# Attention and a gated feed-forward block in one kernel: output groups of seven 384-column products instead of two times seven 192-column ones

## The chip, the cores and the metric

The kernel runs on one core of a Trainium2 chip. The metric is device time in microseconds; the time given for a kernel is the median of its runs. Engines that matter here: TensorE (PE: matrix products, whose results lie in PSUM), VectorE (DVE), ScalarE (ACT), GpSimd (POOL) and SyncE (SP, whose queue issues most stores and all transposing transfers).

## The reference

Eight batches of twelve heads, 448 tokens, head size 64, go through softmax attention; the result, 3584 tokens of width 768, goes through a feed-forward block with two input weights of 768 x 1536 and one output weight of 1536 x 768.

```python
def _attn_ref(q, k, v):
    scores = (1.0 / np.sqrt(q.shape[-1])) * np.matmul(q, k.transpose(0, 1, 3, 2))
    attn = np.exp(scores - np.max(scores, axis=-1, keepdims=True))
    attn = attn / (np.sum(attn, axis=-1, keepdims=True) + 1e-09)
    return np.matmul(attn, v)

def _moe_ref(x, w_gate, w_val, w_out):
    g = x @ w_gate
    silu = g * (1.0 / (1.0 + np.exp(-g)))
    return silu * (x @ w_val) @ w_out
```

Inputs and output are float32; the kernel multiplies in float16 and accumulates in float32.

## The kernel before

**Stages.** Attention works on 48 pairs of heads. For each pair TensorE forms transposed scores (tile `s`, L346 to L376), ScalarE takes their exponential into `E` (L366, L384), and TensorE multiplies by the values with a column of ones (tile `acc`, L402 to L438). VectorE divides (`pv_close`), and the 128-column results are turned into `X`, by SP's transposing DMAs for the later pairs (`turn_x`, L525 and L529). A second stream, the feed-forward block, is laid between: its tokens come in blocks of 384 and 512 by turns. A *step* (`class Step`) is one of the twelve 128-row slices of the hidden layer for a block: six products for the gate (`gp`, L588), a tanh on ScalarE (`sg`, L615), six products for the value (`vp`), two VectorE operations (L641, L647) that write `hts`. The last block of 512 and the last 896 tokens use `Unit`, in which the same products are done by Winograd's form of Strassen's method, with seven half-size products in place of eight; an ordering planner (`order_of`) puts those in line.

**Output groups.** The output product, `hts` times `wo`, is done for most tokens by the same seven-product scheme. A *pair* is two chunks of 128 tokens. Its 2 x 2 blocks are (first or second chunk) x (first or second half of the 1536 hidden rows) on the left, and on the right (half of the hidden rows) x (two column ranges). The sums of the left blocks are made by VectorE (`h_sums`, L571 to L574, in `Hall`), those of the right blocks once (`out_sums`, in `Tsum`). Before the change the 768 output columns are taken as two *groups* (`qw` 0 and 1) of 384 columns, each of whose 2 x 2 blocks has 192 columns. `out_group` (L699 and on) runs one: all of its products are 128 x 192 (L710), and their accumulators `a`, `c` and `b` lie in one tile `og` of the `ps_s` pool, `a` and `c` in its first bank and `b` in its second. Each of the seven products is six matmuls. Around them:

- ScalarE (or VectorE, if `own`) copies `a` to `p1` (L754, L756), VectorE adds `c` to give `p15` (L757);
- VectorE writes `p15 + b` back to `c` (L759), reads the next `b` with `p15` to `osb` (L763), and the last `b` with `p1` (L773);
- ScalarE copies `a` and `c` together to `osb` (L735); `store` (L671) issues the DMAs, for the whole 768 columns when the second group ends.

`out_group` is a generator with two stops, so that the callers lay other work in: `run_group` a step inside, `run_groups` two groups of a pair in turn.

**Order.** Everything is written out by hand: instructions stand on each engine in the order of the calls. The loop over `plan` makes visits of three score tiles each, then the values of a pair that is due (in most visits), then feed-forward work. From visit `base` on, the list `VISITS` tells it: (block that begins, steps, groups, plain output slices, sums on VectorE at the end). A visit without values is called bare. Two steps at the end of a visit are run as `run_pair`, with the last one's value in two halves. `sums` is a queue of VectorE operations, taken one at a time by `add_sum`.

PSUM has two pools: `ps_s` with three buffers of two banks (scores, gates, groups) and `ps_f` with two of one bank (value accumulators `acc`, `vp`, plain outputs `op`). A buffer is handed out again in turn when its last reader is done.

After the visits come the last pair of heads, the units of the last block of 512 (`x5`), then three pairs of groups (one left over and `groups5`), the units of the last 896 tokens, and three final pairs, the last of which (`last`) stores each piece as soon as it is there, over two queues.

Of the kernel before, what the change touches and what calls it, by code (L numbers as in the profile page):

```python
# [16 lines left out]
HS = 4096.0  # L17
# [48 lines left out]
def kernel(  # L66
# [487 lines left out]
    def out_sums(c):  # L554
        b11, b12, b21, b22 = (
            wo_all[:, :, ds(f, 2), ts(i, QW)].rearrange("p h c m -> p c h m") for f in (c, NH + c) for i in range(2)
        )
        t1, t2, t3, t4 = (t[:, ds(c, 2)].rearrange("p c (h m) -> p c h m", h=2) for t in Tsum)
        return [
            lambda: nc.vector.tensor_sub(t1, b12, b11),  # L560
            lambda: nc.vector.tensor_sub(t2, b22, t1),
            lambda: nc.vector.tensor_sub(t3, b22, b12),
            lambda: nc.vector.tensor_sub(t4, b21, t2),
        ]
# [138 lines left out]
    def out_group(kk, c0, hts, t, at, qw, osb, last=False, own=False, mid=None):  # L703
        x, y, w = ts(2 * t, 128), ts(2 * t + 1, 128), ts(qw, QW)
        g = ps_s.tile([128, 2, 512], FP32, tag="s", name="og")
        a, c, b = g[:, 0, 0:QW], g[:, 0, QW:OH], g[:, 1, 0:QW]

        def product(dst, lhs, rhs, first=False):
            return [
                nc.tensor.matmul(  # L710
                    dst, lhsT=lhs(n), rhs=rhs(n), start=first and n == 0, stop=n == NH - 1, skip_group_check=True
                )
                for n in range(NH)
            ]

        def hh(half, z):
            return lambda n: hts[:, half * NH + n, z]

        def hs(m):
            return lambda n: Hall[at][m][:, n]  # L720

        def bb(oh, half):
            return lambda n: wo[qw][:, half * NH + n, ts(oh, QW)]

        def tt(m):
            return lambda n: Tsum[m][:, n, w]

        def out_part(z, src):
            if last and qw:
                halves = [osb[z][:, ds(qw * OH + x * QW, QW)] for x in range(2)]  # L730
                return [
                    nc.scalar.activation(halves[0], src[:, 0:QW], AF.Copy, scale=1.0 / HS),
                    nc.vector.tensor_scalar_mul(halves[1], src[:, QW:], 1.0 / HS),
                ]
            return [nc.scalar.activation(osb[z][:, ts(qw, OH)], src, AF.Copy, scale=1.0 / HS)]  # L735

        def stored(z, lo=0, w=OH):
            l0 = c0 + (2 * t + z) * 128
            if last:
                store(osb[z], kk, l0, 128, qw * OH + lo, w, (nc.sync, nc.scalar), True)  # L740
            elif qw and not lo:
                store(osb[z], kk, l0, 128, 0, DM)

        def apart(mms, *others):
            for mm in mms:
                for other in others:
                    tc.declare_no_dep(mm.ins, other.ins, reason="another bank")

        product(a, hh(0, x), bb(0, 0), True)
        product(c, hh(0, y), tt(0))  # L750
        p1 = fp.tile([128, QW], FP32, tag="p1", name="p1")
        p15 = fp.tile([128, QW], FP32, tag="p15", name="p15")
        if own:
            keep1 = nc.vector.tensor_scalar_mul(p1[:], a, 1.0 / HS)  # L754
        else:
            keep1 = nc.scalar.activation(p1[:], a, AF.Copy, scale=1.0 / HS)  # L756
        keep15 = nc.vector.scalar_tensor_tensor(p15[:], c, 1.0 / HS, p1[:], ALU.mult, ALU.add)  # L757
        apart(product(b, hs(0), tt(1), True), keep1, keep15)
        nc.vector.scalar_tensor_tensor(c, p15[:], HS, b, ALU.mult, ALU.add)  # L759
        yield  # L760
        product(b, hs(1), tt(2))
        d = osb[1][:, ds(qw * OH + QW, QW)]
        part = nc.vector.scalar_tensor_tensor(d, b, 1.0 / HS, p15[:], ALU.mult, ALU.add)  # L763
        if last:
            stored(1, QW, QW)
        if mid:
            mid()
        apart(product(a, hh(1, x), bb(0, 1)), part)
        apart(product(c, hs(2), bb(1, 1)), part)
        row0 = out_part(0, g[:, 0, 0:OH])  # L770
        stored(0)
        apart(product(b, hh(1, y), tt(3)), *row0)
        nc.vector.scalar_tensor_tensor(osb[1][:, ds(qw * OH, QW)], b, 1.0 / HS, p1[:], ALU.mult, ALU.add)  # L773
        stored(1, 0, QW if last else OH)
        yield

# [145 lines left out]
    with tc.manual_schedule():  # L922
# [50 lines left out]
        def pair_groups(kk, c0, hts, t, last=False, at=None):  # L973
            at = t if at is None else at
            osb = []

            def begin(qw, own=False, mid=None):
                if not qw:
                    osb.extend(new_osb() for _ in range(2))
                return out_group(kk, c0, hts, t, at, qw, osb, last, own, mid)  # L980

            return [(lambda own=False, mid=None, qw=qw: begin(qw, own, mid), h_sums(hts, t, at) if not qw else []) for qw in range(2)]

        def add_block(i, visits):
# [18 lines left out]
            groups.extend(x for t in range(1 + odd) for x in pair_groups(kk, c0, hts, t))  # L1003
# [3 lines left out]
            sums.extend(groups[0][1])  # L1007
            later = [f for _, fs in groups[1:] for f in fs]
            groups[:] = [(begin, []) for begin, _ in groups]
            sums.extend(later)  # L1010

# [3 lines left out]
            (2, 2, 0, 0, 2), (0, 2, 0, 0, 3), (0, 1, 1, 0, 0), (0, 2, 0, 0, 0), (0, 1, 1, 0, 0),  # L1015
            (0, 2, 0, 0, 0), (0, 1, 1, 0, 0), (0, 2, 0, 0, 0), (0, 1, 1, 0, 0), (3, 2, 0, 0, 1),
            (0, 2, 0, 0, 1), (0, 1, 1, 0, 0), (0, 0, 0, 1, 0), (0, 2, 0, 0, 0), (0, 0, 0, 1, 0),
            (0, 1, 1, 0, 0), (0, 0, 0, 1, 0), (0, 2, 0, 0, 0), (0, 0, 0, 1, 0), (0, 2, 0, 0, 0),
            (4, 2, 0, 0, 1), (0, 2, 0, 0, 1), (0, 1, 1, 0, 0), (0, 1, 0, 0, 0), (0, 1, 1, 0, 0),
            (0, 1, 0, 0, 0), (0, 1, 1, 0, 0), (0, 1, 0, 0, 0), (0, 1, 1, 0, 0), (0, 1, 0, 0, 0),  # L1020
# [84 lines left out]
        def run_group(nf, inside=None, gate_first=False, sum_between=True):  # L1105
            gen = groups.pop(0)[0](gate_first)
            for _ in range(nf - 1):
                run_fv()
            step = fvq.pop(0)
            if gate_first:  # L1110
                step.gate()
                add_sum()
            next(gen)
            if not gate_first:
                step.gate()
                add_sum(sum_between)
            if inside:
                inside()
                next(gen)
            step.value(0)  # L1120
            step.finish()
            if not inside:
                next(gen)
            add_sum()
# [367 lines left out]
```

## Time and profile before

| | |
|---|---|
| median of 3 runs | 427.63 us (427.6 to 427.68) |
| the profiled execution's own time | 427.29 us |
| its span, first to last instruction | 425.5 us |
| PE busy | 419.2 us, 4796 matmuls |
| output groups on PE (L710) | 924 matmuls |
| DVE, ACT, POOL busy | 271.1, 244.9, 229.8 us |
| stage from the first group to the last visit | 133.58 to about 298 us |
| three pairs behind the units of the last 512-block | 327.75 to 348.4 us |
| three final pairs | 400.3 to 421.3 us |

The columns of the profile's rows: line of the kernel, engine, operation, output and input tiles (buffer numbers left out), shape, and `xN` for N instructions merged into one row. In a timeline each row begins with its start and its length in us; in the chain of waits likewise, by engine, tile and line. "PEld" is the loading of a matmul's stationary operand, which overlaps the products. A matmul's end is modelled, so that the lengths of neighbours overlap; the distance between starts is what a product costs TensorE.

### The profile page before, as it was taken

What the parts mean: (1) busy time and instruction counts of PE and PEld (TensorE: products, weight loads), DVE (VectorE), ACT (ScalarE), POOL (GpSimd) and SP (SyncE); (2) the same over time, 40 slices, a digit from 0 to 9 for tenths busy, and PEclk for the clock granted to TensorE, in tenths of its full rate; (3) what the DMA queues carried; (4) which work ended last, traced back from release to release, by engine and by line L of the source; (5) the groups of instructions that cost most, each with busy time, mean ns of one, the idle gap of its engine ahead of it and who ended that gap; (6) DMA issues with size and microseconds to landing.
All of it is one profiled execution on the core that took longest, in us unless ns stands there. A gap on an engine that the chain in (4) does not pass through costs nothing.

```text
span 425.5 us, 11944 instructions
## 1 busy us (share of the span) xinstructions
PE 419.2 (99%) x4796; PEld 292.0 (69%) x4796; DVE 271.1 (64%) x644; ACT 244.9 (58%) x395; POOL 229.8 (54%) x351
## 2 busy tenths in 40 slices
PE   8999999999999999999999999999999999999996
PEld 3766666655557777757766777777889985555795
DVE  4666572785669656575635776677777765665663
ACT  6975667646755654656666546559654235545221
POOL 8656614997887774468733876935999000000000
PEclk9999999999999999999999999999999999999999
DMA  9999999999999999999999998723101231000125
GB/s 136 182 200 200 199 175 190 136 177 215 115 138 143 124 176 121 141 146 129 119 148 136 151 144 106 139 46 94 23 2 29 87 114 36 0 2 1 39 75 149
DMA packets 107928, 49.79 MB, mean 117 GB/s; under 512 B 59872, under 2 KB 104672, under 8 KB 107872
## 3 DMA queue, kind: packets, MB, share of 16 engines
q0 software_dynamic: 46800, 24.56, 52.3%
q1 hardware_dynamic: 60752, 24.22, 30.9%
q8 instruction: 37, 0.61, 0.6%
q10 hardware_dynamic: 320, 0.25, 0.2%
q14 instruction: 19, 0.16, 0.1%
HBM read 49.55 MB, written 11.01 MB: 142 GB/s over the span
## 4 chain that ended last, share of the span: by engine, by line
PE 92%; ACT 4%; DVE 2%; DMA 0%; issue 0%; ACTq 0%; DVEq 0%
PE og L710 17%; PE gp L588 17%; PE vp L588 12%; PE un L833 10%; PE acc L438 8%; PE ub L833 8%; PE s L346 5%; PE op L681 5%; PE acc L402 2%; PE s L376 2%; ACT E L366 2%; PE s L358 1%; ACT E L384 1%; PE tp L317 1%; PE wp L164 1%; PE op L1039 1%
## 5 line engine op out<-in xcount | busy, mean ns | idle before, releaser
L366 ACT ACTIVATE E<-s 128x896 f16<-128x896 f32 x126 | 106.6, 918 | 40.2 <-PE s L346 28.3
L588 PE MATMUL gp<-X,wg 128*128 128x384 f16 (+1 forms) x360 | 74.0, 347 | 0.0
L238 POOL COPY qk<-qkraw 128x512 f16<-128x512 f16 x70 | 43.4, 666 | 55.2 <-DMA qkT<-qk 55.0
L588 PE MATMUL vp<-X,wv 128*128 128x384 f16 (+3 forms) x360 | 66.7, 321 | 0.1
L641 DVE SCALAR_TENSOR_TENSOR t<-sg,gp 128x384 f32<-128x384 f32 (+1 forms) x60 | 36.1, 607 | 41.7 <-ACT sg L615 41.6
L588 PEld LDWEIGHTS <-wv 128*128 128x128 f16 x462 | 43.7, 98 | 25.8 <-issue 0.3
L588 PEld LDWEIGHTS <-wg 128*128 128x128 f16 x360 | 32.8, 98 | 26.2 <-issue 1.9
L178 POOL DMA_DIRECT2D vraw<-in_v_dram x72 | 44.3, 643 | 9.4 <-DVE X L523 8.5
L615 ACT ACTIVATE sg<-gp 128x384 f32<-128x384 f32 (+1 forms) x60 | 32.1, 537 | 27.9 <-PE gp L588 27.4
L178 POOL DMA_DIRECT2D qkraw<-in_k_dram x70 | 42.8, 631 | 6.5 <-DMA wo<-in_moe_w_out_dram 4.0
L384 ACT ACTIVATE E<-s 112x896 f16<-112x896 f32 x48 | 40.5, 917 | 7.9 <-PE s L376 7.8
L438 PEld LDWEIGHTS <-E 128*128 128x128 f16 (+2 forms) x1224 | 38.0, 98 | 10.1 <-issue 4.0
L710 PEld LDWEIGHTS <-hts 128*128 128x128 f16 x528 | 44.1, 98 | 0.3
L438 PE MATMUL acc<-vo,E 128*128 128x65 f16 (+2 forms) x1224 | 42.4, 193 | 0.1
L647 DVE SCALAR_TENSOR_TENSOR hts<-t,vp 128x384 f16<-128x384 f32 (+3 forms) x60 | 32.5, 541 | 5.8 <-PE vp L588 1.9
L481 DVE TENSOR_TENSOR xt<-acc,R 128x256 f16<-128x256 f32 x72 | 30.6, 425 | 2.5
L735 ACT ACTIVATE osb<-og 128x384 f32<-128x384 f32 x21 | 10.3, 490 | 37.9 <-PE og L710 37.9
L201 POOL DMA_DIRECT2D qkraw<-in_q_dram x43 | 29.6, 688 | 4.3 <-DMA vraw<-in_v_dram 1.4
L346 PE MATMUL s<-qkT 64*64 64x448 f16 (+1 forms) x288 | 30.8, 354 | 0.4
L710 PE MATMUL og<-wo,hts 128*128 128x192 f16 x264 | 29.0, 246 | 0.0
L710 PEld LDWEIGHTS <-hsum 128*128 128x128 f16 x300 | 25.6, 98 | 1.0
L219 DVE COPY vo<-vraw 128x512 f16<-128x512 f16 (+1 forms) x48 | 21.8, 457 | 3.0 <-DMA vraw<-in_v_dram 2.9
(184 smaller groups left out, 708.8 us busy)
## 6 DMA issues: line engine op xcount, KB each, us to landing
vraw<-in_v_dram POOLq DMA_DIRECT2D x72, 64.0 KB, 4.9
qkraw<-in_q_dram POOLq DMA_DIRECT2D x39, 112.0 KB, 4.2
qkraw<-in_k_dram POOLq DMA_DIRECT2D x68, 64.0 KB, 4.7
wg<-in_moe_w_gate_dram POOLq DMA_DIRECT2D x8, 288.0 KB, 9.8
wv<-in_moe_w_val_dram POOLq DMA_DIRECT2D x8, 288.0 KB, 10.4
wo<-in_moe_w_out_dram POOLq DMA_DIRECT2D x2, 1152.0 KB, 19.2
out_dram<-osb SPq DMA_DIRECT2D x7, 288.0 KB, 3.7
out_dram<-osb SPq DMA_DIRECT2D x6, 336.0 KB, 3.4
```

The costliest lines, as they stand in the source:

```text
L178: eng.dma_start(dst[ts(s, 64)], rows)
L238: nc.gpsimd.tensor_copy(dst.rearrange("p c h d -> p h c d"), src)
L346: nc.tensor.matmul(s[ts(half, m), hx, 0:S], lhsT=t[ts(hx, 64), ds((c + low(pr, hx)) * 128 + half * m, m)], rhs=t[ts(hx, 64), ds(NC * 128, S)],
L366: nc.scalar.activation(e[:, 0 : 2 * S].rearrange("p (h q) -> p h q", h=2), s[:, :, 0:S], AF.Exp, scale=sm_scale)
L384: nc.scalar.activation(e[:, :, 0:S], s[0:P, :, 0:S], AF.Exp, scale=sm_scale)
L438: nc.tensor.matmul(acc[ds(lo, m), ts(j, D + 1)], lhsT=e[rows, ds(hx * S + j * 128 + lo, m)], rhs=Vts[pr % NV][rows, hx, col, 0 : D + 1], s ...
L588: nc.tensor.matmul(dst[:, 0:w], lhsT=wslice(kind, self.fb, cb), rhs=X[kk][:, cb, ds(c0 + lo, w)], start=(cb == 0), stop=(cb == NCB - 1),)
L615: self.readers = [nc.scalar.activation(self.sg[:, 0:n], gp[:, 0:n], AF.Tanh, scale=0.5)]
L641: nc.vector.scalar_tensor_tensor(self.t1[:, 0:n], self.sg[:, 0:n], 1.0, self.gp[:, 0:n], ALU.add, ALU.mult)
L647: nc.vector.scalar_tensor_tensor(self.hts[:, self.fb, ds(lo, w)], self.t1[:, ds(lo, w)], 0.5 * HS, vp[:, 0:w], ALU.mult, ALU.mult)
L710: nc.tensor.matmul(dst, lhsT=lhs(n), rhs=rhs(n), start=first and n == 0, stop=n == NH - 1, skip_group_check=True)
L833: mm = nc.tensor.matmul(dst, lhsT=lhs[:, n], rhs=rhs[:, n], start=first and n == 0, stop=n == NK - 1, skip_group_check=True,)
```

## The change

All groups become wide ones: a pair is one group, whose 2 x 2 blocks have 384 columns. `out_group` and `pair_groups` give way to a class `OutPair` with a method `wide`; accumulators `a` and `c` have a bank each in one `ps_s` tile, and `b` lies in a `ps_f` buffer (in the last pair in two halves, in a second `ps_s` tile). `p1` and `p15` have 384 columns, one buffer each in the visits, and the tiles `kept` at the end. Nothing is laid inside a group but up to four VectorE sums. In `VISITS`, five visits hold a group and no step, and five that held a group now have no group and one step more; the visits' totals of steps are the same. The early opening of value accumulators behind a group (`after_group`) goes, and so does the variant with values inside a group (`run_group_with`). `out_sums` pairs the columns as halves of 384.

```diff
@@ out_sums
-        b11, b12, b21, b22 = (
-            wo_all[:, :, ds(f, 2), ts(i, QW)].rearrange("p h c m -> p c h m") for f in (c, NH + c) for i in range(2)
-        )
-        t1, t2, t3, t4 = (t[:, ds(c, 2)].rearrange("p c (h m) -> p c h m", h=2) for t in Tsum)
+        b11, b12, b21, b22 = (wo[i][:, ds(f, 2)] for f in (c, NH + c) for i in range(2))
+        t1, t2, t3, t4 = (t[:, ds(c, 2)] for t in Tsum)
@@ out_group -> OutPair.wide
-        g = ps_s.tile([128, 2, 512], FP32, tag="s", name="og")
-        a, c, b = g[:, 0, 0:QW], g[:, 0, QW:OH], g[:, 1, 0:QW]
...
+        def wide(self, keep, add_sum, ns=(1, 2, 1)):
+            osb = self.open()
+            g = ps_s.tile([128, 2, 512], FP32, tag="s", name="og")
+            a, c = g[:, 0, 0:OH], g[:, 1, 0:OH]
+            if self.last:
+                bs = ps_s.tile([128, 2, 512], FP32, tag="s", name="ob")
+                parts = [(i * QW, QW, bs[:, i, 0:QW]) for i in range(2)]
+            else:
+                parts = [(0, OH, ps_f.tile([128, 512], FP32, tag="f", name="ob")[:, 0:OH])]
...
+            product(a, self.hh(0, self.x), self.bb(0, 0, 0, OH), True)
+            keep1 = nc.scalar.activation(p1, a, AF.Copy, scale=1.0 / HS)
+            apart(product(c, self.hh(0, self.y), self.tt(0, 0, OH), True), keep1)
+            done = [nc.vector.scalar_tensor_tensor(p15, c, 1.0 / HS, p1, ALU.mult, ALU.add)]
+            for lo, w, b, mms in products(self.hs(0), 1, True):
+                done.append(combine(c, p15, HS, b, lo, w))
+            add_sum(ns[0])
+            apart(product(a, self.hh(1, self.x), self.bb(0, 1, 0, OH)), *done)
+            left = nc.scalar.activation(osb[0][:, 0:OH], a, AF.Copy, scale=1.0 / HS)
...
+            if self.last:
+                self.stored(0, 0, OH, both)
+            for lo, w, b, mms in products(self.hs(1), 2):
+                combine(osb[1][:, OH:], b, 1.0 / HS, p15[:, ds(lo, w)], lo, w)
+            if self.last:
+                self.stored(1, OH, OH, both)
+            add_sum(ns[1])
+            apart(product(c, self.hs(2), self.bb(1, 1, 0, OH)), left)
+            nc.scalar.activation(osb[0][:, OH:], c, AF.Copy, scale=1.0 / HS)
...
+            for lo, w, b in parts:
+                mms = product(b, self.hh(1, self.y), self.tt(3, lo, w))
+                apart(mms, *ends)
+                ends.append(combine(osb[1], b, 1.0 / HS, p1[:, ds(lo, w)], lo, w))
+                if self.last:
+                    self.stored(1, lo, w, both)
+            if not self.last:
+                self.stored(1)
+            add_sum(ns[2])
@@ VISITS
-            (2, 2, 0, 0, 2), (0, 2, 0, 0, 3), (0, 1, 1, 0, 0), (0, 2, 0, 0, 0), (0, 1, 1, 0, 0),
-            (0, 2, 0, 0, 0), (0, 1, 1, 0, 0), (0, 2, 0, 0, 0), (0, 1, 1, 0, 0), (3, 2, 0, 0, 1),
-            (0, 2, 0, 0, 1), (0, 1, 1, 0, 0), (0, 0, 0, 1, 0), (0, 2, 0, 0, 0), (0, 0, 0, 1, 0),
-            (0, 1, 1, 0, 0), (0, 0, 0, 1, 0), (0, 2, 0, 0, 0), (0, 0, 0, 1, 0), (0, 2, 0, 0, 0),
-            (4, 2, 0, 0, 1), (0, 2, 0, 0, 1), (0, 1, 1, 0, 0), (0, 1, 0, 0, 0), (0, 1, 1, 0, 0),
-            (0, 1, 0, 0, 0), (0, 1, 1, 0, 0), (0, 1, 0, 0, 0), (0, 1, 1, 0, 0), (0, 1, 0, 0, 0),
+            (2, 2, 0, 0, 2), (0, 2, 0, 0, 3), (0, 0, 1, 0, 0), (0, 2, 0, 0, 0), (0, 2, 0, 0, 0),
+            (0, 2, 0, 0, 0), (0, 0, 1, 0, 0), (0, 2, 0, 0, 0), (0, 2, 0, 0, 0), (3, 2, 0, 0, 1),
+            (0, 2, 0, 0, 1), (0, 0, 1, 0, 0), (0, 0, 0, 1, 0), (0, 2, 0, 0, 0), (0, 0, 0, 1, 0),
+            (0, 2, 0, 0, 0), (0, 0, 0, 1, 0), (0, 2, 0, 0, 0), (0, 0, 0, 1, 0), (0, 2, 0, 0, 0),
+            (4, 2, 0, 0, 1), (0, 2, 0, 0, 1), (0, 0, 1, 0, 0), (0, 1, 0, 0, 0), (0, 2, 0, 0, 0),
+            (0, 1, 0, 0, 0), (0, 0, 1, 0, 0), (0, 1, 0, 0, 0), (0, 2, 0, 0, 0), (0, 1, 0, 0, 0),
             (5, 0, 0, 1, 0), (0, 0, 0, 2, 0), (0, 0, 0, 0, 0),
@@ run_group
+        def run_group():
+            pair = groups.pop(0)
+            keep = [fp.tile([128, OH], FP32, tag=tag, bufs=1, name=tag) for tag in ("p1", "p15")]
+            pair.wide(keep, add_sum, (1, 1, 0))
@@ score tiles of a visit
-                if n == 2 and (after_group or ordered[n] in quads):
+                if n == 2 and ordered[n] in quads:
                     rests = open_products(rests, small)
@@ the groups behind the units
-                one, two = (begin(mid=add_sum) for begin, _ in pair)
-                next(one)
-                add_sum()
-                for gen in (two, one, two):
-                    next(gen)
-                add_sum()
+            for n, pair in enumerate(pairs):
+                pair.wide(kept[2 * (n % 2) : 2 * (n % 2) + 2], add_sum)
```

## The prediction

> **What bounds the kernel now.** I read the page's busy line, its slices and its chain first, and then the timeline of the stages where the output groups stand.
>
> ```profile
> PE 419.2 (99%) x4796; PEld 292.0 (69%) x4796; DVE 271.1 (64%) x644; ACT 244.9 (58%) x395; POOL 229.8 (54%) x351
> PE   8999999999999999999999999999999999999996
> PEclk9999999999999999999999999999999999999999
> PE 92%; ACT 4%; DVE 2%; DMA 0%; issue 0%; ACTq 0%; DVEq 0%
> PE og L710 17%; PE gp L588 17%; PE vp L588 12%; PE un L833 10%; PE acc L438 8%; PE ub L833 8%; PE s L346 5%; PE op L681 5%; PE acc L402 2%; PE s L376 2%; ACT E L366 2%; PE s L358 1%; ACT E L384 1%; PE tp L317 1%; PE wp L164 1%; PE op L1039 1%
> ```
>
> TensorE is in hand at full granted clock, and 92% of the chain is its work; the output groups (og, L710) are the largest line of it. So there are only three ways to move the time: fewer nanoseconds for the same products, less waiting of TensorE, or a shorter end. The chain of waits gives the pace of narrow products and of 384-column ones, here from two stages:
>
> ```profile
> 152.86 1.95 PE gp L588 x12
> 327.75 20.79 PE og L710 x252
> ```
>
> 20.79/252 = 82.5 ns for 192 columns, 1.95/12 = 162.5 ns for 384. Two narrow ones cost 165.0, so a wide one saves 2.5 ns; and 252 in a row at that pace means that the groups themselves wait for nothing today. The small waits stand behind them. TensorE's timeline, first behind a narrow group, then behind a pair of steps, then in a visit with a single step:
>
> ```profile
> 138.50 0.66 PE L710 MATMUL og<-qkraw,hts 128*128 128x192 f16 x6
> 139.09 0.38 PE L358 MATMUL s<-qkT 64*64 64x448 f16 x4
> 139.30 0.76 PE L346 MATMUL s<-qkT 64*64 64x448 f16 x8
> 139.99 2.12 PE L588 MATMUL gp<-X,wg 128*128 128x384 f16 x12
> ...
> 176.46 0.55 PE L346 MATMUL s<-qkT 64*128 64x448 f16 x4
> 176.85 0.28 PE L438 MATMUL acc<-vo,E 64*128 64x65 f16 x8
> 177.05 0.36 PE L346 MATMUL s<-qkT 64*128 64x448 f16 x2
> 177.34 0.91 PE L438 MATMUL acc<-vo,E 128*128 128x65 f16 x24
> 178.09 1.24 PE L588 MATMUL gp<-X,wg 128*128 128x512 f16 x5
> ```
> ```profile
> 169.41 0.74 PE L346 MATMUL s<-qkT 64*128 64x448 f16 x6
> 169.99 1.12 PE L438 MATMUL acc<-vo,E 64*128 64x65 f16 x32
> 170.95 0.25 PE L710 MATMUL og<-wo,hts 128*128 128x192 f16 x1
> ```
>
> Behind a pair of steps, scores and values take 169.41 to 170.95 = 1.54 us; behind a narrow group 176.46 to 178.09 = 1.63. In the visit without values, scores take 139.09 to 139.99 = 0.90 against 0.59 in others (0.21 for L358, 0.38 for the eight of L346): the second and third score tiles wait for the narrow group's and the step's PSUM tiles.
>
> **The change, part by part.**
>
> *The products.* Eleven pairs of token chunks, two narrow groups each, 7 products of 6 matmuls: 924 narrow. After: ten pairs of 42 wide, and the last pair, whose three T products are in halves, 24 wide and 36 narrow. 924 x 82.5 = 76.23 us; 444 x 162.5 + 36 x 82.5 = 75.12. All of it is on the path: **-1.1 us**, 0.53 of it in the five pairs of the visits, 0.58 in the six at the end.
>
> *Inside a wide group.* The b bank is written three times, with one product of another bank (6 x 162.5 = 0.975 us) between uses, in which VectorE must read it. No 384-wide combine of this kind stands in the trace; the nearest rows are L641 and L647, the same operation at 384 columns, 553 ns (192-wide combines 353 to 363). A product's modelled end lies 0.163 behind the next product's start (0.246 long, 0.0825 spacing), VectorE began 0.04 behind that (419.13 + 0.66 to 419.83), and TensorE 0.04 behind VectorE (268.22 to 268.26). So the return is 0.163 + 0.04 + 0.553 + 0.04 = 0.80 of 0.975: hidden, 0.18 to spare. Ahead of it in VectorE's order stand the two closings of the values (2 x (0.176 + 0.425) = 1.2 us, done about 1.05 behind the group's start by the rows at 255.59); the token sums (0.55) are emitted behind a combine and are done before the next one is due. ScalarE's first copy can come behind the third exponential, at about 1.4, ends at 1.9, and p15 is due at 2.15. I take 0, with 0.1 a return (20 returns, 2 us) as the far bound; a gain is excluded, as the groups wait for nothing now.
>
> *The visits.* Ten visits held a step and a narrow group or so (2, 4, 6, 8, 11, 15, 22, 24, 26, 28 of the list VISITS, counted from 0; 2 begins at 132.0, 28 at 278.7); now 2, 6, 11, 22, 26 hold a group alone and 4, 8, 15, 24, 28 have one step more. The same 12 steps of each block remain. Visits that followed a narrow group and now follow a pair of steps (5, 9, 16, 25, 29) should take 1.54 instead of 1.63: 0.09 each. Visit 3 loses its 0.31, because the group's tile now holds only a and c, and c is copied out (0.49) while the last product (0.975) runs. Visits 7, 12, 23, 27 follow a wide group: b now lies in the two-buffer pool that the value accumulators use, so the second accumulator waits for b's last combine, free at 0.80 behind the last product, where scores are through at 0.09 + 0.58 + 0.03 = 0.70 (0.09: the four products before 139.09 take 2.08, not 1.98). That is 0.10, about the 0.09 that these visits waste today. In 16, 25 and 29 the next thing late is ScalarE (chain of waits, in the visit after a group):
>
> ```profile
> 264.28 2.41 ACT E L366 x3
> 266.69 0.04 issue
> 266.74 0.50 ACT sg L615
> 267.24 0.02 issue
> 267.26 0.56 DVE t L641
> 267.83 0.02 issue
> 267.85 0.37 DVE hts L647
> ```
>
> Three exponentials, the gate's tanh and two VectorE operations set when the next score tile is free (268.26); TensorE arriving 0.09 earlier waits 0.09 longer. So I count 0.31 + 2 x 0.09: **-0.5 us**, between 0 and the 1.1 that ten visits waste today (0.31 + 9 x 0.09).
>
> *Stores and VectorE's other work.* Each pair's eight or so stores on SP now go out one to four visits earlier. Behind them in SP's order stand the transposes of keys and values; a burst of four stores took 2.6 us (264.66), while the last key transpose is issued at 275.08, lands about 5 later and is first read at 292.84. That cover of over 10 us hides it. Per pair VectorE falls from 8 x 0.357 to 4 x 0.553 us and ScalarE from 1.65 to 1.47: neither on the path. The weight sums keep their sizes and their order: nothing.
>
> *The end.* VectorE and the stores behind the last product:
>
> ```profile
> 420.62 0.66 PE L710 MATMUL og<-qkraw,hts 128*128 128x192 f16 x6
> ...
> 421.41 0.36 DVE L733 TENSOR_SCALAR osb<-og 128x192 f32<-128x192 f32 x1 [1.22 <-DMA out_dram<-osb]
> 421.68 0.35 DVE L773 SCALAR_TENSOR_TENSOR osb<-og,p 128x192 f32<-128x192 f32 x1
> ```
>
> The last product ends at 421.28, its combine begins at 421.68 behind L733, which waited for a store, and the last of the stores goes out near 422.2, 0.92 behind the product. After, L733 is gone (ScalarE copies 384 columns while the last halves of b are multiplied): combine from 0.04 to 0.40, store at 0.43; the store before it, at about -0.07, takes some 0.4 of each queue and does not hold it. **-0.45 us**, between 0 and 0.5.
>
> **Sum:** -1.1 - 0.5 - 0.45 = -2.05 us. The profiled execution took 427.29 (span 425.5 and 1.8 around it), 0.34 under the median of 427.63; 425.2 on its own scale is 425.6 on the median's.
>
> **Rivals.**
>
> *The chain through ScalarE eats the visits.* If, as in visit 25 (from 263.88), exponentials pace most visits from 2 to 29, TensorE's 0.53 + 0.5 there become waits: -0.58 - 0.45 = -1.0, 426.6. For it: three of the visits are paced so. Against: a group visit gives 6.8 us of products to 2.5 of exponentials, and a pair visit 3.9 or more.
>
> *The b bank turns round too slowly* (slower). If anything stands ahead of the combine on VectorE when b is ready, say one token sum of 0.55, the return is 1.35 and TensorE waits 0.38; at 20 returns 7.5 us, 433.1. It decides from a return of 1.08 on (20 x 0.10 eats the 2.05). For it: narrow groups had a step or a second group between their halves, and this cover is gone. Against: the order of emission puts sums behind the combines, and the margin of 0.18 is a third of an operation.
>
> The Trainium skill speaks for that rival twice, in Perfetto Trace Analysis: under Optimizing Tensor Performance, independent groups should rotate through banks so that reading one overlaps the products of the next, and under Optimizing Scalar/DVE Operations, breaking instructions up can let work finish sooner where VectorE or ScalarE cause TensorE's bubbles. The trace so far has no bubble in the narrow groups and gives the 0.18 above, so that by these rules the sum would be the rival's, and by the rows it stays at -2.05.
>
> *Nothing to be measured.* Twenty returns late by 0.05 and the four visits behind wide groups waiting 0.2 instead of 0.1 give back 1.4 of the 2.05: 427.0.
>
> **How the numbers follow.** 0.2% (0.86 us) is about what a measurement of this kernel can tell from no change. Forecast 0.60, its own range 424.6 to 426.2; the chain through ScalarE 0.19; nothing 0.08; the slow bank 0.13. The first two are faster: 0.79. The low end of the range takes all bounds at their best (-1.1 - 1.1 - 0.5 = -2.7) and 0.4 more for prices too high, 424.5; the high end takes in the second case and most of the third, 427.3. Outside are the slow bank and a little at each end, under 0.2.
>
> **What would show it.** Right: L710's successor with 480 matmuls, wide ones at 162.5 ns in unbroken runs of 42; visit 3's scores at 0.59; the last store about 0.45 behind the last product. Wrong: gaps of TensorE ahead of the second or third product into ob; values behind a wide group waiting more than 0.2 for VectorE; exponentials back to back over several visits; or a key transpose that lands after its visit has begun.

## The result, and the profile after

The change makes the kernel faster by 0.3%: 426.31 us (median of 11 runs, 425.87 to 427.19) against 427.6 for the kernel before on the same chip (11 runs, 427.05 to 427.89). The ratio is 0.9971, 95% interval 0.9962 to 0.998, that is 0.9 to 1.6 us. The forecast was 425.6. The direction was right, and the time lies in the whole range of 424.5 to 427.3, but 0.1 outside the forecast's own part of it (424.6 to 426.2), on the side of its first rival; the gain of 2.05 us was forecast too large by 0.8. The profiled execution took 426.09 us, its span 424.31, 1.19 less than the span before.

The page of the kernel after, with the busy line, the clock and the chain:

```profile
PE 417.6 (98%) x4382; PEld 263.7 (62%) x4382; DVE 265.2 (63%) x606; ACT 243.5 (57%) x385; POOL 229.6 (54%) x351
PEclk9999999999999999999999999999999999999999
PE 93%; ACT 3%; DVE 2%; DMA 1%; issue 1%; SPq 0%; DVEq 0%; ACTq 0%
```

TensorE has 1.6 us less work and still bounds the kernel at the full granted clock. The chain of waits in the three pairs behind the units, where no other work lies between:

```profile
327.30 1.95 PE og L703 x12
329.25 0.97 PE ob L703 x6
330.23 0.98 PE og L703 x6
...
334.13 1.95 PE og L703 x12
```

A wide product takes 162.5 ns (0.975 for six), and three b products alternate with the others without a gap: a group takes 6.83 us here. The next table lays the stages of both profiled executions side by side, measured from the starts of the first matmuls.

| stage | before | after | measured | forecast |
|---|---|---|---|---|
| start to the first group | 133.58 | 133.60 | 0 | 0 |
| first group to the units of the last 512-block | 164.58 | 164.10 | -0.48 | -0.53 products, -0.5 waits |
| three pairs behind those units | 20.79 | 20.47 | -0.32 | with the next but one, -0.58 |
| both stretches of units, 29.4 and 51.95 | 81.37 | 81.39 | +0.02 | 0 |
| first to last matmul start of the final pairs | 20.71 | 20.47 | -0.24 | (above) |
| last matmul's start to VectorE's end | 1.00 | 0.64 | -0.36 | -0.35 |
| VectorE's end to the end of the span | 3.47 | 3.63 | +0.16 | -0.1 |

So the products gave what they should, the visits' small waits gave nothing in sum, and the end gave less than half. TensorE's timeline of the kernel after shows the visits: behind the first wide group, through the visit without values and its pair of steps, to the next scores and values.

```profile
139.45 1.14 PE L703 MATMUL ob<-qkraw,hts 128*128 128x384 f16 x6
140.52 0.38 PE L358 MATMUL s<-qkT 64*64 64x448 f16 x4
140.73 0.55 PE L346 MATMUL s<-qkT 64*64 64x448 f16 x8
141.21 2.12 PE L586 MATMUL gp<-X,wg 128*128 128x384 f16 x12
...
145.23 0.86 PE L346 MATMUL s<-qkT 64*128 64x448 f16 x6
145.92 1.19 PE L438 MATMUL acc<-vo,E 64*128 64x65 f16 x32
146.94 0.81 PE L586 MATMUL gp<-X,wg 128*128 128x384 f16 x4
```

Scores in the visit without values take 140.52 to 141.21 = 0.69 (0.90 before): a gain, though not down to the 0.59 of the forecast. But scores and values of the next visit take 145.23 to 146.94 = 1.71, where the same visit took 1.54 before (144.01 to 145.55). Summed over all visits of this stage, the times of scores and values come to the same 47.45 us before and after. The gains, 0.69 together (-0.21 here, -0.08 to -0.09 each in visits 5, 9, 16 and 29, the rest in small pieces), are paid back in others: +0.18 in visit 4 and +0.06 to +0.09 in each of 15, 17, 25 and 30, 0.48 together, and +0.04 to +0.06 in each of the four behind wide groups (7, 12, 23 and 27), 0.20 together. Visits are counted from 0 at the first entry of `VISITS`; TensorE's part of a visit begins with its scores.

### The profile page after: what moved, and what is told of

It reads as the page before. It is cut to its first block, busy times and chain, and to the rows that moved or that the text cites. A ratio compares the mean times of both kernels' runs of the same rounds, so it can differ in the third digit from the quotient of the medians.

```text
span 424.3 us, 11026 instructions
## 1 busy us (share of the span) xinstructions
PE 417.6 (98%) x4382; PEld 263.7 (62%) x4382; DVE 265.2 (63%) x606; ACT 243.5 (57%) x385; POOL 229.6 (54%) x351
## 4 chain that ended last, share of the span: by engine, by line
PE 93%; ACT 3%; DVE 2%; DMA 1%; issue 1%; SPq 0%; DVEq 0%; ACTq 0%
PE gp L586 18%; PE vp L586 12%; PE un L855 10%; PE og L703 10%; PE acc L438 8%; PE ub L855 8%; PE ob L703 8%; PE s L346 5%; PE op L679 4%; PE acc L402 2%; PE s L376 2%; ACT E L384 1%; PE s L358 1%; ACT E L366 1%; PE tp L317 1%; PE op L1049 1%
## 5 line engine op out<-in xcount | busy, mean ns | idle before, releaser
L238 POOL COPY qk<-qkraw 128x512 f16<-128x512 f16 x70 | 42.8, 655 | 57.3 <-DMA qkT<-qk 56.0
L586 PE MATMUL gp<-X,wg 128*128 128x384 f16 (+1 forms) x360 | 73.1, 348 | 0.0
L586 PE MATMUL vp<-X,wv 128*128 128x384 f16 (+3 forms) x360 | 64.2, 314 | 0.1
L586 PEld LDWEIGHTS <-wv 128*128 128x128 f16 x492 | 46.1, 98 | 24.5 <-issue 0.4
L703 PEld LDWEIGHTS <-hts 128*128 128x128 f16 x270 | 25.9, 98 | 15.9
L645 DVE SCALAR_TENSOR_TENSOR hts<-t,vp 128x384 f16<-128x384 f32 (+3 forms) x60 | 31.4, 523 | 5.6 <-PE vp L586 2.1
L481 DVE TENSOR_TENSOR xt<-acc,R 128x256 f16<-128x256 f32 x72 | 30.6, 425 | 2.5
L201 POOL DMA_DIRECT2D qkraw<-in_q_dram x43 | 29.4, 685 | 4.2 <-DMA vraw<-in_v_dram 1.5
L346 PE MATMUL s<-qkT 64*64 64x448 f16 (+1 forms) x288 | 29.2, 353 | 0.5 <-DVE hts L645 0.2
L703 PE MATMUL og<-wo,hts 128*128 128x384 f16 x132 | 25.1, 326 | 0.0
L480 DVE RECIPROCAL R<-acc 128x4 f32<-128x4 f32 x72 | 12.7, 177 | 17.7 <-PE acc L438 17.5
L219 DVE COPY vo<-vraw 128x512 f16<-128x512 f16 (+1 forms) x48 | 19.7, 413 | 3.4 <-DMA vraw<-in_v_dram 3.4
L679 PE MATMUL op<-wo,hts 128*128 128x192 f16 (+1 forms) x168 | 21.4, 281 | 0.0
```

Of the source, the lines that this page charges most:

```text
L238: nc.gpsimd.tensor_copy(dst.rearrange("p c h d -> p h c d"), src)
L346: nc.tensor.matmul(s[ts(half, m), hx, 0:S], lhsT=t[ts(hx, 64), ds((c + low(pr, hx)) * 128 + half * m, m)], rhs=t[ts(hx, 64), ds(NC * 128, S)],
L586: nc.tensor.matmul(dst[:, 0:w], lhsT=wslice(kind, self.fb, cb), rhs=X[kk][:, cb, ds(c0 + lo, w)], start=(cb == 0), stop=(cb == NCB - 1),)
L679: nc.tensor.matmul(op[:, 0:w], lhsT=hts[:, fb, ts(ch, 128)], rhs=wo[oh][:, fb, ds(off, w)], start=fb == 0, stop=fb == NFB - 1,)
L703: nc.tensor.matmul(dst, lhsT=lhs(n), rhs=rhs(n), start=first and n == 0, stop=n == NH - 1, skip_group_check=True)
```

## The experiments

**Wide sums, narrow products.** Everything as after, but each wide product is issued as two of 192 columns.

```diff
     def product(dst, lhs, rhs, first=False):
+        w = dst.shape[1]
+        step = min(w, QW)
         return [
             nc.tensor.matmul(
-                dst, lhsT=lhs(n), rhs=rhs(n), start=first and n == 0, ...
+                dst[:, ds(lo, step)], lhsT=lhs(n), rhs=rhs(n)[:, ds(lo, step)],
+                start=first and n == 0 and lo == 0, ...
             )
+            for lo in range(0, w, step)
             for n in range(NH)
```

> The changed kernel with each wide product issued as twice six 192-column matmuls into the same accumulators; order, VISITS, VectorE and ScalarE work, PSUM tiles and stores are those of the changed kernel. Theory (the gain is 2.5 ns for each matmul saved, and the new arrangement of the visits is worth nothing): 444 wide matmuls become 888 narrow ones, 444 x (165.0 - 162.5) = +1.1 us over the changed kernel, about 427.4; the lead over the kernel before at the end of the visits, 0.40 us, falls to about 0; what is left of the gain is the end, 0.2 us. Rival (the gain comes from the arrangement, from fewer waits and fewer VectorE and ScalarE operations): no more than 0.2 us slower than the changed kernel, about 426.4, and the lead of 0.40 stays.

Measured: 428.3 us (427.99 to 429.62), ratio to the kernel before 1.0018 (1.0006 to 1.0029). In the stages against the kernel after: visits +0.54, three pairs +0.32, final pairs +0.26, together 1.1, which is the 444 x 2.5 ns of the forecast; a group in the visits takes 7.02 instead of 6.92. The visits' stage is then 164.64, against 164.58 in the kernel before: with narrow products the new arrangement of the visits is worth nothing. The span is 2.22 longer than that of the kernel after (426.53 against 424.31), and the other 1.1 us of this lie elsewhere: 0.38 ahead of the first group, a stretch that differed by up to 0.65 between the profiled executions of all these kernels, and some 0.7 behind the last matmul, where SP's and ScalarE's queues were held longer by their stores. ScalarE's two stores behind the last group's first half, of this kernel and then of the kernel after:

```profile
419.34 2.25 ACTq L669 DMA_DIRECT2D out_dram<-osb  x2
```

```profile
417.85 1.54 ACTq L669 DMA_DIRECT2D out_dram<-osb  x2
```

The last copy of c stands behind them in ScalarE's order, and they took 2.25 instead of 1.54. Why is not settled. The product term of the forecast is confirmed where it was placed.

**Values in halves behind a wide group.** The second accumulator waits there for b's last combine; that wait has cover if the values are taken as in the visits ahead of the first group: the first accumulator's full rows, then the last rows of both, then the second's full rows, and not the last rows of both first.

```diff
-            split = 0 <= base - x < 3
+            split = 0 <= base - x < 3 or (x > base and VISITS[x - 1 - base][2] > 0)
```

> The changed kernel, but in a visit behind a wide group the values of the first head are multiplied into the first accumulator before the second accumulator is touched. Theory (the 0.12 us that the values lose behind a wide group are the second accumulator's wait for the last combine of b; behind that, exponentials pace the visits with a plain output slice or a single step): scores and values of visits 7, 12, 23 and 27 fall from 1.71, 1.71, 1.66 and 1.67 us to about 1.55 to 1.6; the visits behind 12 and 27 give their share back, so that the lead at the end of the visits grows by 0.1 to 0.25 us, and the time to about 426.1. Rival (the 0.12 is a cost of switching from products to scores and values, not a wait): no visit changes by over 0.03 us.

Measured: 426.88 us (426.0 to 430.45), ratio 0.9987 (0.9966 to 1.0007): no gain. The four visits became 1.75 to 1.77 instead of 1.66 to 1.71, 0.29 us more together. TensorE's timeline in one of them, here and then in the kernel after:

```profile
165.39 0.55 PE L346 MATMUL s<-qkT 64*64 64x448 f16 x8
165.87 1.24 PE L438 MATMUL acc<-vo,E 128*128 128x65 f16 x32
166.94 0.81 PE L586 MATMUL gp<-X,wg 128*128 128x384 f16 x4
```

```profile
165.19 0.55 PE L346 MATMUL s<-qkT 64*64 64x448 f16 x8
165.58 1.27 PE L438 MATMUL acc<-vo,E 64*64 64x65 f16 x40
166.68 1.14 PE L586 MATMUL gp<-X,wg 128*128 128x384 f16 x6
```

In the kernel after, the matmul that opens the second accumulator at 165.70 comes 118 ns behind the one ahead of it, when b's combine (VectorE, 165.09 to 165.65) is through. That wait, forecast as 0.10, is gone in the split form. But the split form changes between matmuls over 64 rows and over 128 rows twice more, and each change shows as 121 to 125 ns between two starts. The wait was as forecast, but this cure costs more than it saves: neither the theory (1.55 to 1.6) nor the rival (no change) came about.

**The last stores.** The last pair's second half goes out as one 384-column store behind both combines, not as two.

```diff
-                if self.last:
-                    self.stored(1, lo, w, both)
-            if not self.last:
+            if self.last:
+                self.stored(1, 0, OH, both)
+            else:
                 self.stored(1)
```

> The changed kernel, but the last row block's left half is stored by one pair of DMAs behind both halves instead of a pair behind each. Theory (the last store is held by its queue, which issues one per 0.4 to 0.47 us, and not by the combine): the last pair of stores goes out within 0.1 us of the end of the last combine (0.15 to 0.25 in the changed kernel), and the end comes 0.05 to 0.15 us earlier in spite of twice the bytes. Rival (the end is set by how long the last store takes to land): later by 0.1 us or more, as 147 KB instead of 74 KB land last.

Measured: 426.47 us (425.98 to 428.28), ratio 0.9971 (0.9956 to 0.9986), the same as the kernel after. The last store is issued 0.03 us behind the last combine instead of 0.23, but the last landing comes 2.42 behind that issue instead of 2.18, and the span ends 3.81 behind VectorE instead of 3.63. So the queue's hold is real, some 0.2, and a larger last transfer takes it back and 0.18 more, which is the rival's sign; this is one profile of each, and the medians do not tell the two kernels apart.

Its profile showed something else, in the first wide group: 7.27 us instead of 6.92. The chain of waits there:

```profile
134.98 0.54 DVE qkraw L569
...
135.64 0.43 DVE xt L481
...
136.12 1.15 PE ob L703 x6
```

The first product into b waits for the closing of a value accumulator (L481), because b takes its buffer. VectorE came to it late, since two sums ahead of it were long. Its rows, and GpSimd's:

```profile
132.68 0.89 DVE L570 TENSOR_TENSOR hts<-hts 128x768 f16<-128x768 f16 x1
133.60 0.85 DVE L571 TENSOR_TENSOR hsum<-hts 128x768 f16<-128x768 f16 x1
134.48 0.56 DVE L572 TENSOR_TENSOR hsum<-hts,hsum 128x768 f16<-128x768 f16 x1
```

```profile
132.54 1.49 POOL L238 COPY qk<-qkraw 128x512 f16<-128x512 f16 x2 [3.15 <-DMA qkT<-qk]
```

In the kernel after, the same sums take 0.55 and 0.56, and GpSimd's copies lie before them (130.47 to 131.64).

**Half of the exponentials' work.** To see whether ScalarE's chain ate the visits' gain, the exponentials of the later stages cover half their columns, in both kernels; the other half of the attention weights is left out.

```diff
+        w = S if len(ering) <= ER else S // 2
         nc.scalar.activation(
-            e[...].rearrange("p (h q) -> p h q", h=2), s[:, :, 0:S], AF.Exp, scale=sm_scale
+            e[...].rearrange("p (h q) -> p h q", h=2)[:, :, 0:w], s[:, :, 0:w], AF.Exp, scale=sm_scale
```

> The kernel before with each exponential of the pairs from the thirteenth on (L366) taken over half of its columns: half of the attention weights are left out, and ScalarE needs about 0.57 us instead of 0.92 for each. All theories: waits of TensorE for score tiles behind the single steps (about 0.3 us each, three times) and behind the plain output slices (0.1 to 0.25 us each) shrink or go; those behind narrow groups, 0.09 us each, stay; 1 to 3 us faster than the kernel before. It is there for the comparison with the changed kernel under the same cut.

> The changed kernel with the same cut: each exponential of the pairs from the thirteenth on over half of its columns, so half of the attention weights are left out. Theory (the exponentials' chain took what the new arrangement of the visits would have given: 0.18 and 0.08 us behind the bare visits with a pair of steps, 0.06 to 0.09 behind plain output slices and single steps): with ScalarE's work halved these go, and the lead over the kernel before under the same cut, at the end of the visits, is 0.7 to 0.9 us instead of 0.40; the whole difference 1.5 to 1.8 us. Rival (the visits' gain never existed: TensorE's own switching costs and VectorE's return time are the same): the lead at the end of the visits is 0.35 to 0.5 us as before the cut, the whole difference 1.2 us.

> The changed kernel with each exponential of the pairs from the thirteenth on over half of its columns, so half of the attention weights are left out; profiled once more, since the first profile was at half the granted clock and tells nothing of the visits. Against the kernel before under the same cut, the theory (the exponentials' chain took the visits' gain) wants a lead of 0.7 to 0.9 us at the end of the visits, and the 0.18 us behind visit 3 and the 0.08 behind visit 24 gone; the rival (that gain never existed) a lead of 0.35 to 0.5 and the same 0.18 and 0.08.

Measured: before with the cut 427.16 us (426.94 to 428.1), ratio to the whole kernel before 0.9987 (0.9976 to 0.9997), which is 0.6 us and not the expected 1 to 3; after with the cut 425.5 beside it (ratio 0.9947, 0.993 to 0.9964) and 425.4 in a second comparison (0.995, 0.9936 to 0.9963), whose profile is read here. Without the exponentials' length the change is worth 427.16 - 425.5 = 1.66 us instead of 1.29. The intervals are too wide to tell these two apart; the visits do. Their stage falls from 164.21 to 163.12, by 1.09 instead of 0.48. Of this 0.51 are the times of scores and values (46.98 against 46.47 us), which without the cut gained nothing; about 0.1 stands in the first group's visit of the kernel before, which took 5.60 instead of 5.51 in this profile. Counted from the start of the span the lead is only 0.64, under the expected 0.7 to 0.9, since the first group began 0.45 later in this profile of the kernel after. TensorE's timeline with the cut, where the kernel after had 1.71:

```profile
145.58 0.74 PE L346 MATMUL s<-qkT 64*128 64x448 f16 x6
146.16 1.12 PE L439 MATMUL acc<-vo,E 64*128 64x65 f16 x32
147.12 1.14 PE L587 MATMUL gp<-X,wg 128*128 128x384 f16 x6
```

145.58 to 147.12 is 1.54, so the loss of 0.18 in visit 4 is gone, and that of 0.08 in visit 25 too (1.54); visits 15, 17 and 30 are the same in both cut kernels. The visits behind wide groups keep their 1.66 to 1.71, as they should, since b's combine and not ScalarE is late there. ScalarE's own rows say how it comes about, of the kernel after and of the cut one:

```profile
140.98 2.54 ACT L366 ACTIVATE E<-s 128x896 f16<-128x896 f32 x3 [0.84 <-PE s L358]
143.38 0.90 ACT L613 ACTIVATE sg<-gp 128x384 f32<-128x384 f32 x2
145.64 1.73 ACT L366 ACTIVATE E<-s 128x896 f16<-128x896 f32 x2 [1.36 <-PE s L346]
```

```profile
141.33 1.42 ACT L367 ACTIVATE E<-s 128x448 f16<-128x448 f32 x3 [0.84 <-PE s L358]
142.75 0.49 ACT L614 ACTIVATE sg<-gp 128x384 f32<-128x384 f32 x1
143.72 0.49 ACT L614 ACTIVATE sg<-gp 128x384 f32<-128x384 f32 x1 [0.48 <-PE gp L587]
```

Uncut, three exponentials run to 143.5 and both gates' tanhs follow back to back behind them; cut, the second tanh waits 0.48 for TensorE, so that ScalarE has time to spare. VectorE's rows of the kernel after show what TensorE waits for in visit 4:

```profile
145.33 0.35 DVE L645 SCALAR_TENSOR_TENSOR hts<-t,gp 128x192 f16<-128x192 f32 x1
145.59 0.35 DVE L645 SCALAR_TENSOR_TENSOR hts<-t,vp 128x192 f16<-128x192 f32 x1
```

They read the two halves of the last step's value: the first half lies in the `ps_s` buffer of its gate, the second in a `ps_f` buffer. The first ends at 145.68, and the third score tile starts at 145.73, 0.11 late; the second ends at 145.94, and the second value accumulator is opened at 146.00, 0.07 late. Before the change they ended at 144.25 and 144.51, and the third score tile started at 144.40 without a wait; with the cut the first ends at 145.55, ahead of 145.97. So with its scores 0.21 earlier, TensorE comes to the next visit's score tiles before the chain of exponentials, tanh and VectorE has set them free.

**Sums behind the closings.** If late closings were part of what is missing, fewer VectorE sums ahead of them would help.

```diff
-            (2, 2, 0, 0, 2), (0, 2, 0, 0, 3), (0, 0, 1, 0, 0), ...
+            (2, 2, 0, 0, 2), (0, 2, 0, 0, 1), (0, 0, 1, 0, 0), ...
-            (4, 2, 0, 0, 1), (0, 2, 0, 0, 1), (0, 0, 1, 0, 0), ...
+            (4, 2, 0, 0, 1), (0, 2, 0, 0, 0), (0, 0, 1, 0, 0), ...
         def run_group():
             pair = groups.pop(0)
+            add_sum(sum(f in sums for f in pair.todo))
```

> The changed kernel with up to two of VectorE's token sums, which stood ahead of the closings of the values in the visits with the first and the fourth wide group, emitted behind those closings. Theory (in some executions these sums fall on GpSimd's copies, take 0.85 to 1.0 us instead of 0.55, and the closings behind them give b's buffer back so late that TensorE waits 0.05 to 0.35 us at the first product into b): no group of the visits takes over 6.95 us of TensorE, whatever the sums take, and the median is 0.1 to 0.3 us under the changed kernel, ratio to the kernel before 0.9964 to 0.9969. Rival (the long groups come from late data or a late exponential): groups of 7.0 to 7.3 us appear here too, and the ratio stays at 0.9971 or above.

Measured: 426.28 us (425.87 to 426.48), ratio 0.9965 (0.9952 to 0.9979), not to be told from the kernel after. All its groups take 6.92, but in its profile these sums take 0.55 to 0.56, none lengthened by a GpSimd copy, so it does not tell the theories apart.

**Late closings on purpose.** In both kernels, one weight sum is done again four times with the same values, ahead of the closings in the visits 2, 6, 11, 22 and 26.

```diff
+            for _ in range(4 if x - base in (2, 6, 11, 22, 26) else 0):
+                out_sums(0)[3]()
             for _, p0 in todo:
                 if split:
```

> Four VectorE sums of 0.48 us each (one of the weight sums, done again with the same values) stand ahead of the values' closings in the five visits with a wide group; nothing is left out. The first closing ends in the changed kernel 0.35, 1.48, 1.48, 1.34 and 1.47 us before the first product into b is due (135.20 against 135.55, 158.53 against 160.01, and so on). Theory, that b hangs on the closings because it lies in the value accumulators' pool: the closings come 1.93 us later where VectorE has no idle time ahead of them (the groups at 133.6 and 248.2) and about 1.25 later at the others (0.64 to 0.70 of idle time). So TensorE waits 1.93 - 0.33 = 1.6 in the first group, 0.6 in the fourth and nothing in the other three: 2.2 us more, 428.5, with groups of 8.5, 6.92, 6.92, 7.5 and 6.92. Rival, that the late sums were seen beside the wait by chance and b's place does not matter: all five stay at 6.92, 426.3.

> The same four sums in the same five visits of the kernel before, whose groups have b in their own tile. Theory: a narrow group asks nothing of the closings, and its first combine has the step's products behind it as cover, so the time stays at that of the kernel before, 427.6, within 0.6. Rival, that VectorE itself is short there, whatever the place of b: slower by about as much as the changed kernel is with them, 2 us, 429.6.

Measured: after with late closings 436.27 us (434.14 to 438.71), ratio 1.0194 (1.0146 to 1.0243); before with them 434.28 (433.67 to 436.5), ratio 1.0157 (1.0118 to 1.0195); the kernel before took 428.3 beside them. Both expectations were far off. The mechanism held in the kernel after: all five groups wait at their first product into b, and for L481. TensorE's rows from three of them:

```profile
138.28 1.30 PE L703 MATMUL ob<-E,hsum 128*128 128x384 f16 x6 [2.08 <-DVE xt L481]
139.37 2.13 PE L703 MATMUL og<-wo,hts 128*128 128x384 f16 x6
...
165.56 1.15 PE L703 MATMUL ob<-E,hsum 128*128 128x384 f16 x6 [0.96 <-DVE xt L481]
...
281.80 1.46 PE L703 MATMUL ob<-E,hsum 128*128 128x384 f16 x6 [3.11 <-DVE xt L481]
```

The groups take 10.85, 8.06, 7.47, 8.19 and 11.89 us instead of 6.92. Two sizes were wrong. The four sums took 2.3 to 4.8 us instead of 1.93: they write the same tile, each waits for the one ahead of it, so that they start 0.59 apart where nothing else is in the way, and beside GpSimd's work some took longer still, up to 1.26. And behind the two longest waits TensorE ran slowly: six wide products in 1.92 us (139.58 to 141.50 in the chain) instead of 0.975. Those slow products cost 1.7 us more in each of these two groups. The windows of the first group give the granted clock (the third column from the end):

```profile
136.00:138.00 2.00, 0.20 (x2) 0.00 (x0) 1.90 (x5) 0.00 (x0) 0.94 (x2) 1.00 1.48 134
...
139.40:141.30 1.90, 1.90 (x8) 0.89 (x7) 1.02 (x2) 0.00 (x0) 0.47 (x1) 0.50 0.37 67
```

In the kernel before, the narrow products kept their pace, apart from two groups whose second part took 2.20 and 2.43 instead of 2.07, but the step laid inside them waited:

```profile
137.60 1.15 PE L588 MATMUL vp<-X,wv 128*128 128x384 f16 x6 [1.28 <-DVE xt L481]
```

The step's value product `vp` takes a buffer of the same pool as b does now, and waited 1.28, 1.70 and 1.47 us for the closings in three visits. The visits' stage grew by 6.9 us there and by 12.2 in the kernel after, by the profiles (that of the kernel after is of the slowest of its four executions); in the medians the intervals of the two overlap. That late closings cost time wherever b lies, the rival of the second expectation, is what came about; that b hangs on them is shown by the rows alone. So the narrow kernel hangs on the closings as well, only later in the visit: three narrow products and the step's gate product, 1.48 + 0.98 us, stand ahead of `vp`, where two wide products, 1.95 us, stand ahead of b.

## Why the prediction was right in direction and 0.8 us too large

*The products (-1.1).* Right. -0.45 in the visits' groups (five times 0.09, as 5.51 + 5.51 became 6.92 + 4.01), -0.32 and -0.24 at the end: -1.0, and the first experiment puts +1.1 back in the same three places.

*Inside a wide group (0).* Right in the kernel after's profile: 6.92 us in all five and no gap ahead of the second or third product into b. What the step said of the first product, closings "done about 1.05 behind the group's start", held in four groups (1.02 to 1.16); in the first they were done 2.15 behind it. There the closing that b waits for ends at 135.20, 0.35 before b is due, and in two of the experiments' profiles (groups of 7.27; of 6.99 and 7.10) it came too late. How much of the median this costs is open; it is at most a few tenths of a microsecond, by these lengths.

*The visits' waits (-0.5).* This step failed. The terms named in it were there: visits 5 and 9 gained 0.08 and 0.09, visit 3 gained 0.21 (0.31 was counted from a floor of 0.59, but the same scores take 0.69 where nothing is late). What the step said of visits 16, 25 and 29 alone, that TensorE arriving earlier waits longer for ScalarE's chain, is what happened in visit 4 (+0.18), 25 (+0.08) and, less clearly, 15, 17 and 30; 16 and 29 gained. A second loss, 0.20, stands in the four visits behind wide groups, which the step took as even. The sum over the stage is nothing: 0.69 gained, 0.48 lost to the chain, 0.20 behind wide groups. The cut of the exponentials takes the chain's 0.48 away, so that cause is shown. That 0.51 are then gained, the step's 0.5, is in part luck: 0.39 come from the three visits that it named, 0.27 from 16, 25 and 29, of which it expected nothing, 0.20 are lost behind wide groups, and the rest is in small pieces. The loss to the chain is the forecast's first rival, in half its size: this rival put the products' 0.53 at risk too, and these came through.

*The end (-0.45).* Less than half came: 0.20. VectorE ended 0.36 sooner behind the last matmul's start, for the reason given: `L733` is gone. The step that failed is that the store ahead of the last one "takes some 0.4 of each queue and does not hold it". The rows of the kernel after:

```profile
419.13 1.15 PE L703 MATMUL ob<-qkraw,hts 128*128 128x192 f16 x12
...
419.82 0.85 DVE L760 SCALAR_TENSOR_TENSOR osb<-ob,kept 128x192 f32<-128x192 f32 x2 [0.85 <-PE ob L703]
```

The last combine ends at 420.68. Its last store goes out 0.23 later, where the step had 0.03; in the kernel before it was 0.24 already (422.27 behind 422.03), so the hold is not new, it only did not go away. The last landing is 2.18 behind that issue instead of 2.06, and 0.07 more lies behind the landing than before. Why is open, and some of it is scatter: from VectorE's end to the end of the span it is 3.50 to 3.63 in five profiles with the new end and 3.47 to 3.53 in three with the old, about 0.1 apart and not 0.16.

*The slow bank (rival, 0.13).* It did not come about in the kernel after. Its two points hold in part: a sum or two ahead of VectorE's work is enough to stop TensorE, but at the first use of b, through the closings, and not at b's returns.

## What to carry to other kernels

When a small wait is taken from an engine, look for what is late next at that very place, and ask it of every place where the wait goes, not of those alone where the trace already names it: here 0.5 us of waits went from PSUM to ScalarE's chain. An accumulator that moves into a shared pool inherits the waits of that pool's other readers; take the margin to its first use from the timeline, with the operations ahead of that reader at their longest seen length. A store issued just before the last one sets when the last can go out: where the trace before shows such a hold (0.24 here), do not count on its going away.

## What was not expected of the hardware

*VectorE's sums under GpSimd's work.* A sum of 768 float16 columns, both inputs and the result in SBUF, took 0.54 to 0.56 us alone. Of 70 that ran beside GpSimd's copies L238 for 0.3 us or more, in the profiles of all these kernels, 37 took 0.8 to 1.06, 17 stayed under 0.6, 8 lay between, and 8 took 1.16 to 1.74. With GpSimd's own sums beside it, in the kernel with late closings, three in a row took 1.16 to 1.19 in the chain of waits:

```profile
276.46 1.19 DVE qkraw L561
...
277.68 1.16 DVE qkraw L561
...
278.86 1.16 DVE qkraw L561
```

GpSimd's sums L818 to L821 took up to 1.22 in this stretch and 0.91 behind it. The Trainium skill, SBUF — State Buffer, section SBUF: two separate sides, says that VectorE's operations with two SBUF inputs and those of GpSimd's operations that read SBUF share a pair of ports, one holding it for its whole instruction while the other waits. The rows agree in that both grow longer. In the same profiles, of 185 sums with nothing but GpSimd's DMA issues beside them 181 took 0.54 to 0.56.

*The clock behind a wait.* A wait of TensorE of 2.08 us and one of 3.11 were each followed by about 3.4 us at a granted clock of 0.5 (worked out from the windows: 0.91 over 1.4 us, 0.50 over 1.9 and 0.61 over 1.6 in the first; 0.69 over 1.3, 0.50 over 1.9 and 0.74 over 1.4 in the second); waits of 0.96 and 1.09 were not, nor were those of 1.28, 1.47 and 1.70 in the kernel before with late closings, whose windows all show 1.00. The Trainium skill, TensorE: Matmul & The Clock Gate, section What's actually happening, gives half the clock after an idle window of about 3.4 us. The length of the slow stretch agrees with that window; but here a wait of 2.08 us was enough, and the measurement decides.

*A change of shape.* Two neighbouring matmuls, one over 64 rows and one over 128, started 121 to 125 ns apart, in the values of 65 columns, where the 128-row ones among themselves started 29 to 38 apart.
